# Loading q and k in 72-token runs from batch 3 on, so that the copies out of their transposes write unit steps

## The chip, the core and the metric

The kernel runs on one core of a Trainium2 chip. The metric is the device time of one execution in microseconds (us). Executions have a state: "slow" ones are longer at a lower granted TensorE clock, or over 1.5% above the fastest of the same kernel; comparisons here use fast runs. Engines: PE is TensorE (PEld its weight loads), DVE is VectorE, ACT is ScalarE, POOL is GpSimd, SP is SyncE, which issues DMAs here.

## The reference

Causal attention with a bias from a running sum, then a mixer that works first along the tokens (low rank) and then along the channels. Shapes: 8 batches, 8 heads, 576 tokens, head size 64, model width 512, hidden width 2048. Cut to what matters:

```python
scores = scale * q @ k.T                                 # per batch and head, causal
cum    = cumsum(maximum(s, 0), axis=-1)
scores = where(causal, -1e9, scores + minimum(-(cum_i - cum_j), 0))
x      = softmax(scores) @ v                             # heads side by side: (8, 576, 512)
u      = x + (x.T @ U @ V).T                             # mix along the tokens, rank 32
out    = u + maximum(u @ w_ch1, 0) @ w_ch2               # mix along the channels
```

## The kernel before

Heads go in pairs, n = 0..31, four pairs to a batch. For each pair, q and k are loaded with tokens on partitions, transposed by PE into PSUM (four 72x128 pieces per head and tensor; each piece holds two tokens' head rows, one in partitions 0-63 and one in 64-127), and copied as bf16 to `slot`, from which the score matmuls read. There are four such copies for a pair: two heads times two partition halves (`par`).

```python
def load_qk(b, h, n):                       # one run of 8 tokens (2 KB of fp32) per partition and head
    for dst, src in ((q_t[b], q), (k_t[b], k)):
        nc.gpsimd.dma_start(
            out=dst[:, ds(h, n), :],
            in_=src[b, ds(h, n)].rearrange("h (p t) d -> p h (t d)", p=TP),      # TP = 72
        )

def copies(n, hh, par):                     # which engine copies; DVE mostly
    b = n // PB
    on_act = hh == (n == 4) and ((n in (0, 1, 4, 8, 9) or n > 8 and n % PB == 2) or n == 2 and par == 0)
    return nc.scalar.copy if on_act else nc.vector.tensor_copy

def transposes(n):
    ... # cut: bias rows for slot by DMA; 16 PE transposes (line L280) into tps[hh], a PSUM bank per head
        dst = slot[0:D, hh, 0 : 2 * S].rearrange("p (c m t two) -> p c m t two", c=2, t=4, two=2)
        for par in range(2):
            copies(n, hh, par)(             # line L297
                dst[:, :, :, :, par],
                tp[par * D : par * D + D].rearrange("p c t m -> p c m t"),
            )
```

Row p of the load holds tokens 8p to 8p+7. So a transposed piece has every eighth token in its columns, and a copy must interleave: it writes every second bf16 element of `slot` and reads PSUM in steps of 72 elements.

The mixer's matmuls (128x512, lines L608 and L618) are woven between the attention steps in a fixed program order. The mix along the tokens (`seqmix`, L451 to L496) adds `xT`, a transpose of x made by DMA (24 transposes in the trace). All of q, k and v come through one DMA queue, fed by POOL. Loads of batch b+1 are issued once batch b-1's last transposes are done (POOL waits for such transposes four times in the trace of before, 114.1 us in all).

The softmax here doesn't subtract the row's maximum and nothing guards it: scores larger than these inputs give would overflow.

## Time and profile before

| | before |
|---|---|
| time, median of the runs beside after | 376.39 us |
| PE busy, whole span | 368.5 of 374.9 us |
| PE busy, 86 to 300 us (batches 3 to 7, mostly) | 213.46 of 214.00 us |
| `slot` copies, ns each | DVE 802, ACT 801 |
| packets on the DMA queue of q, k, v | 50,880 |

From the page, part 1: busy time of each engine, its share of the span, and its instructions.

```profile
PE 368.5 (98%) x3583; PEld 211.5 (56%) x3583; DVE 213.7 (57%) x446; ACT 200.8 (54%) x301; POOL 69.4 (19%) x108
```

The windows view: length of the window, then for each engine busy us (and instructions), then granted clock, DMA share and GB/s.

```profile
86.00:300.00 214.00, 213.46 (x2213) 124.87 (x2211) 138.37 (x293) 121.52 (x185) 20.41 (x25) 1.00 0.78 89
```

PE is full in the stretch in which the change acts; DVE is busy for 138 us of 214 and ACT for 122. A full PE is not by itself a proof, since matmul ends are modelled and a short wait can hide in them. The timeline agrees with PE as the limit all the same: four 128x512 matmuls hold PE for 0.86 us, and the next group starts at once (four start at 120.64 us, the next group at 121.50).

The view of tile `slot`, its copies (duration in ns as min/median/max, first and last start), and the line of the queue that POOL feeds (packets, MB, share of the time of 16 engines):

```profile
L297 DVE COPY slot<-pwork x105: 780/802/814, 8.2 to 275.2; 64x576 bf16<-64x576 bf16 x105
L297 ACT COPY slot<-pwork x23: 783/801/814, 6.9 to 259.7; 64x576 bf16<-64x576 bf16 x23
```

```profile
q0 software_dynamic: 50880, 18.44, 54.5%
```

### The profile page before, as it was taken

How to read it: one execution, taken by the hardware profiler on the slowest of the kernel's cores; microseconds unless marked ns; L12 is line 12 of the kernel's file. 1: busy time of each engine (PE TensorE's matmuls, PEld its weight loads, DVE VectorE, ACT ScalarE, POOL GpSimd, SP SyncE). 2: the span in 40 equal slices, each digit the busy share in tenths (PEclk: the TensorE clock that was granted, in tenths of full speed). 3: DMA queues.
4: the chain of work that ended last, by engine and by line, in shares of the span. 5: the costliest groups of instructions: out<-in, count | busy, mean ns of one | idle time of the engine just before them, and what ended most of it. 6: DMA issues, size and time to landing. Idle time of an engine off the chain costs nothing.

```text
span 374.9 us, 8505 instructions
## 1 busy us (share of the span) xinstructions
PE 368.5 (98%) x3583; PEld 211.5 (56%) x3583; DVE 213.7 (57%) x446; ACT 200.8 (54%) x301; POOL 69.4 (19%) x108
## 2 busy tenths in 40 slices
PE   8999999999999999999999999999999999999996
PEld 4675666666655556556656665666565544444443
DVE  7876777587668665876477756875573142002011
ACT  3875965757841777067814782368535610621610
POOL 8997436014002300140005000000000000000000
PEclk9999999999999999999999999999999999999999
DMA  7999999999948991699169923220223015302002
GB/s 109 166 206 205 175 173 134 179 124 138 89 55 138 172 78 26 127 164 119 20 117 151 135 34 87 79 63 17 51 81 92 19 35 120 71 30 84 0 30 84
DMA packets 89774, 37.29 MB, mean 99 GB/s; under 512 B 71112, under 2 KB 84136, under 8 KB 89736
## 3 DMA queue, kind: packets, MB, share of 16 engines
q0 software_dynamic: 50880, 18.44, 54.5%
q1 hardware_dynamic: 38856, 18.31, 27.2%
q8 instruction: 28, 0.46, 0.5%
q14 instruction: 10, 0.08, 0.1%
HBM read 37.25 MB, written 9.70 MB: 125 GB/s over the span
## 4 chain that ended last, share of the span: by engine, by line
PE 91%; ACT 4%; DVE 2%; issue 1%; DMA 1%; ACTq 0%; POOLq 0%
PE pwork L618 32%; PE pwork L608 31%; PE pscore L362 10%; PE pwork L422 8%; PE pwork L280 4%; ACT slot L297 2%; PE pscore L324 1%; DVE slot L297 1%; DMA q_sd<-in_q_dram 1%; PE pwork L655 1%; PE pscore L608 1%; ACT pT L388 1%; PE pscore L496 1%; ACT pT L377 0%; PE pwork L362 0%
## 5 line engine op out<-in xcount | busy, mean ns | idle before, releaser
L608 PE MATMUL pwork<-uT,w_sb 128*128 128x512 bf16 x560 | 135.6, 379 | 0.6 <-ACT pT L394 0.2
L618 PE MATMUL pwork<-w_sb,hT 128*128 128x512 bf16 x560 | 135.1, 379 | 0.3 <-DVE slot L297 0.3
L640 ACT ACTIVATE hT<-pwork 128x512 bf16<-128x512 f32 x140 | 84.8, 610 | 73.8 <-PE pwork L608 73.7
L297 DVE COPY slot<-pwork 64x576 bf16<-64x576 bf16 x105 | 84.0, 800 | 10.5 <-PE pwork L280 7.8
L377 ACT ACTIVATE pT<-pscore 128x1024 bf16<-128x1024 f32 x56 | 56.2, 1029 | 60.4 <-PE pscore L362 60.3
L608 PEld LDWEIGHTS <-w_sb 128*128 128x128 bf16 x576 | 51.0, 98 | 50.2 <-issue 1.2
L618 PEld LDWEIGHTS <-hT 128*128 128x128 bf16 x560 | 49.2, 98 | 49.2 <-issue 1.9
L362 PE MATMUL pscore<-slot 68*128 68x320 bf16 (+1 forms) x500 | 54.6, 246 | 0.2
L362 PEld LDWEIGHTS <-slot 68*128 68x128 bf16 x564 | 41.5, 97 | 22.9 <-issue 1.3
L678 DVE TENSOR_TENSOR o_sb<-pwork,u_sd 128x512 f32<-128x512 f32 x31 | 21.4, 689 | 57.3 <-PE pwork L618 56.7
L307 DVE TENSOR_TENSOR pT<-pT,keep 128x512 bf16<-128x512 bf16 (+1 forms) x81 | 28.7, 354 | 39.6 <-ACT pT L394 23.6
L422 PEld LDWEIGHTS <-pT 128*128 128x128 bf16 x870 | 33.1, 98 | 11.0 <-issue 0.3
L422 PE MATMUL pwork<-v_slot,pT 128*128 128x65 bf16 x870 | 35.3, 193 | 0.0
L432 DVE TENSOR_TENSOR x_sb<-pwork,rec 128x320 bf16<-128x320 f32 x64 | 31.5, 492 | 2.2
L107 POOL DMA_DIRECT2D q_sd<-in_q_dram x13 | 10.2, 782 | 117.4 <-PE pwork L280 114.1
L173 POOL DMA_DIRECT2D v_slot<-in_v_dram x36 | 30.4, 864 | 7.3 <-DMA w_sb<-in_moe_w_ch_dram 3.3
L388 ACT ACTIVATE pT<-pscore 128x1024 bf16<-128x1024 f32 x29 | 30.3, 1044 | 1.9 <-PE pscore L362 1.0
L431 DVE RECIPROCAL rec<-pwork 128x5 f32<-128x5 f32 x64 | 12.3, 192 | 24.6 <-PE pwork L422 24.1
L297 ACT COPY slot<-pwork 64x576 bf16<-64x576 bf16 x23 | 18.4, 801 | 7.3 <-PE pwork L280 6.6
L280 PEld LDWEIGHTS <-q_sd 72*128 72x128 bf16 x256 | 14.6, 98 | 9.9 <-DMA q_sd<-in_q_dram 1.0
L280 PE MATMUL pwork<-identity,q_sd 72*128 72x72 bf16 x256 | 18.4, 197 | 0.1
L280 PE MATMUL pwork<-identity,k_sd 72*128 72x72 bf16 x256 | 18.0, 197 | 0.0
(106 smaller groups left out, 194.7 us busy)
## 6 DMA issues: line engine op xcount, KB each, us to landing
out_dram<-o_sb SPq DMA_DIRECT2D x35, 256.0 KB
w_sb<-in_moe_w_ch_dram POOLq DMA_DIRECT2D x4, 1024.0 KB, 13.1
v_slot<-in_v_dram POOLq DMA_DIRECT2D x28, 128.0 KB, 15.8
q_sd<-in_q_dram POOLq DMA_DIRECT2D x5, 576.0 KB, 10.4
k_sd<-in_k_dram POOLq DMA_DIRECT2D x5, 576.0 KB, 14.5
q_sd<-in_q_dram POOLq DMA_DIRECT2D x4, 288.0 KB, 9.0
k_sd<-in_k_dram POOLq DMA_DIRECT2D x4, 288.0 KB, 15.3
q_sd<-in_q_dram POOLq DMA_DIRECT2D x4, 144.0 KB, 5.4
```

The source lines that it names most:

```text
L173: nc.gpsimd.dma_start(out=vt[:rows_t, t, :, 0:D], in_=v[b, :, ds(t * 128, rows_t), :].rearrange("h p d -> p h d"),)
L280: nc.tensor.transpose(tps[hh][:, c, t2, :], src[:, 2 * hp + hh, ds(t2 * 128, 128)], identity[:TP, :TP],)
L297: copies(n, hh, par)(dst[:, :, :, :, par], tp[par * D : par * D + D].rearrange("p c t m -> p c m t"),)
L307: nc.vector.tensor_tensor(dst, dst, keep[:, :, 0:w].to_broadcast([128, n_tiles, w]), op=ALU.min)
L362: nc.tensor.matmul(dst, lhsT=slot[0:KA, hh, ds(S + j * 128, 128)], rhs=slot[0:KA, hh, lo:hi], start=True, stop=True,)
L377: nc.scalar.activation(pT[:, hh, 0:1024], near, EXP, scale=scale)
L388: nc.scalar.activation(pT[:, :, 1024:1536], mid.rearrange("p (a b) -> p a b", a=2), EXP, scale=scale)
L422: nc.tensor.matmul(po[:, i, :], lhsT=pT[:, hh, ds(place(j, i), 128)], rhs=vt[:, j, h, :], start=(j == 0), stop=(j == i), skip_group_check= ...
L432: nc.vector.tensor_tensor(x_sb[:, hp, :, ds(hh * D, D)], po[:, :, 0:D], rec.to_broadcast([128, 5, D]), op=ALU.mult,)
L608: nc.tensor.matmul(f1, lhsT=w1_sb[:, kt, ds(nf * 128, 128)], rhs=u[:, kt, :], start=(kt == 0), stop=(kt == 3),)
L618: nc.tensor.matmul(f2, lhsT=hT[:, nf, ds(i * 128, 128)], rhs=w2_sb[:, nf, :], start=(nf == 0), stop=(nf == NF - 1 and not more), skip_grou ...
L640: nc.scalar.activation(hT[:, nf, :], f1, RELU)
```

## The change

Intent: from batch 3 on, load so that row p holds tokens p, 72+p, 144+p, and so on. Then a transposed piece has 72 consecutive tokens in its columns, and a copy reads and writes unit steps. That VectorE does such a copy faster was the author's assumption, which the trace of before does not show; 454 ns against 802 were measured afterwards. The price: the runs that a load reads shrink from 2 KB to 256 B, so there are eight times as many. Bytes, matmuls and their order stay.

```diff
+    def in_runs(b):
+        return b > 2
+
     def load_qk(b, h, n):
         for dst, src in ((q_t[b], q), (k_t[b], k)):
-            nc.gpsimd.dma_start(
-                out=dst[:, ds(h, n), :],
-                in_=src[b, ds(h, n)].rearrange("h (p t) d -> p h (t d)", p=TP),
-            )
+            if in_runs(b):
+                nc.gpsimd.dma_start(
+                    out=dst[:, ds(h, n), :].rearrange("p h (t d) -> p (h t) d", t=TT),
+                    in_=src[b, ds(h, n)].rearrange("h (t p) d -> p (h t) d", p=TP),
+                )
+            else:
+                ... # as before
@@ transposes
-            dst = slot[0:D, hh, 0 : 2 * S].rearrange("p (c m t two) -> p c m t two", c=2, t=4, two=2)
+            dst = slot[0:D, hh, 0 : 2 * S]
             for par in range(2):
-                copies(n, hh, par)(
-                    dst[:, :, :, :, par],
-                    tp[par * D : par * D + D].rearrange("p c t m -> p c m t"),
-                )
+                src = tp[par * D : par * D + D]
+                if in_runs(b):
+                    by_run = dst.rearrange("p (c t two m) -> p c t two m", c=2, t=4, two=2)
+                    copies(n, hh, par)(by_run[:, :, :, par, :], src)
+                else:
+                    ... # as before
```

More of the change, by code (lines that the diff above doesn't have):

```diff
@@ L103, in alloc_qk @@
         k_t[b] = loads.tile([TP, H, TT * D], BF16, tag="k_sd", name="k_sd")
+    def in_runs(b):
+        return b > 2
     def load_qk(b, h, n):
         for dst, src in ((q_t[b], q), (k_t[b], k)):
-            nc.gpsimd.dma_start(
-                out=dst[:, ds(h, n), :],
-                in_=src[b, ds(h, n)].rearrange("h (p t) d -> p h (t d)", p=TP),
-            )
+            if in_runs(b):
[4 more added lines that the diff above has]
+            else:
+                nc.gpsimd.dma_start(
+                    out=dst[:, ds(h, n), :],
+                    in_=src[b, ds(h, n)].rearrange("h (p t) d -> p h (t d)", p=TP),
+                )
     def ones(ap):
@@ L294, in transposes @@
             tp = tps[hh]
-            dst = slot[0:D, hh, 0 : 2 * S].rearrange("p (c m t two) -> p c m t two", c=2, t=4, two=2)
+            dst = slot[0:D, hh, 0 : 2 * S]
             for par in range(2):
-                copies(n, hh, par)(
-                    dst[:, :, :, :, par],
-                    tp[par * D : par * D + D].rearrange("p c t m -> p c m t"),
-                )
+                src = tp[par * D : par * D + D]
[3 more added lines that the diff above has]
+                else:
+                    in_turn = dst.rearrange("p (c m t two) -> p c m t two", c=2, t=4, two=2)
+                    copies(n, hh, par)(
+                        in_turn[:, :, :, :, par], src.rearrange("p c t m -> p c m t")
+                    )
             yield
```

## The prediction

> **What bounds the kernel.** TensorE. The page gives PE 368.5 us busy of a 374.9 us span at granted clock 1.0. The windows view, from 86 to 300 us (most of batches 3 to 7), has PE busy 213.46 of 214.00 us: 0.54 us idle. The waits view there lists one PE wait (0.2 us, on ACT) and, for weight loads, 0.4 us on a copy of `ux`, none on `slot`. The timeline shows groups following without gaps (four 128x512 matmuls in 0.86 us), so little waiting hides in modelled ends.
>
> **Removed.** The `slot<-pwork` copies (64x576, bf16, PSUM to SBUF) take 802 ns on DVE. For batches 3 to 7 there are 20 head pairs x 4 copies; 10 run on ACT, 70 on DVE. [...] Estimate: the two `o_sb` adds of 128 and 384 elements took 290 and 558 ns, so about 1.05 ns an element[...]. Total: 70 x 0.30 = 21 us of DVE busy, 213.7 -> about 193.
>
> **Added.** Each q or k load of a batch goes from 576 runs of 2 KB (packets of 1024 B written) to 4608 runs of 256 B (128 B written), as v has: 10 loads x 4032 = 40,320 more packets, queue 0 from 50,880 to about 91,200. [...] 1024 B packets ran at about 195 per us, 128 B ones at 450 to 1,200 per us. So q plus k of a batch should take about 18 us (10 to 27) instead of 6 to 8, and the whole load about 28 us instead of 18. PE's instructions are unchanged.
>
> **On the critical path?** Almost none of either. DVE's 21 us lie beside a full PE; at most some tenths of 0.54 us can come back. Loads for batches 4 to 7 are issued at 83, 119, 158 and 196 us; their first transposes are 36 to 45 us later, their values later still, so 28 us fits. Tightest is batch 3: issued at 56 us behind a backlog, packets flow from about 61 us, first transpose at 89 us; I expect q and k by about 80. Longer traffic beside stores and DMA transposes may cost tenths.
>
> **Predicted: 376.2 us, range 375.2 to 378.0; faster by over 2%: 0.01, within 2%: 0.96, slower by over 2%: 0.03.**
>
> **What would show each step.** Right: group `slot<-pwork` on DVE splits into about 35 copies at 802 ns and 70 near 500 ns, ACT's unchanged; DVE busy near 193 us; PE busy still about 368.5; queue 0 near 91,000 packets, its share of the engines up by half or more (54.5% -> 80 to 110%); landing of q and k for batches 3 on 15 to 30 us after issue. Wrong: copies still near 800 ns [...]; PE idle over 1 us between 86 and 300 us; a weight-load wait on q or k at about 89 us.
>
> **What would make it wrong.** Slower: 128 B packets at 350 per us or fewer, so batch 3's k lands after 89 us and stalls PE by some us. Faster: PE waits hidden behind modelled matmul ends that shorter copies release; no room for over 1 us.

The forecast came to 0.30 us less for each copy (802 to about 500 ns), 70 x 0.30 = 21 us less of DVE busy, and 376.2 us. The terms behind the 0.30 us were an assumption that no copy in the trace of before could confirm. The packet rates are of that trace: in single microseconds, 191 to 204 packets of 1,024 B (from 34 to 38 and from 45 to 52 us), and 391 to 1,210 of 128 B (from 39 to 43 and from 68 to 76 us, with packets of other sizes between).

## The result

| | before | after |
|---|---|---|
| time, median | 376.39 us (375.9 to 376.65, 4 runs) | 376.08 us (375.1 to 376.3, 4 runs) |
| ratio of fast runs, 95% interval | | 0.9988 (0.9968 to 1.0009) |
| DVE busy | 213.7 us | 189.5 us |
| `slot` copies from batch 3 on, ns | DVE 802, ACT 801 | DVE 454, ACT 634 |
| packets on the load queue | 50,880 | 104,640 |
| q and k of one batch: issue of q to landing of k (batch 4) | | 18.1 us |

Here and below a ratio is the mean time of one kernel's fast runs over that of the other's of the same rounds, so it is not quite the ratio of the medians.

The time is the same within noise, though every local effect took place. After, in the views shown of before (the new copies have line L309, the old ones L312):

```profile
PE 364.1 (98%) x3524; PEld 210.9 (56%) x3583; DVE 189.5 (51%) x446; ACT 199.1 (53%) x301; POOL 83.5 (22%) x108
```

```profile
L309 DVE COPY slot<-pwork x70: 438/454/460, 89.2 to 272.9; 64x576 bf16<-64x576 bf16 x70
L312 DVE COPY slot<-pwork x35: 786/803/814, 8.2 to 84.4; 64x576 bf16<-64x576 bf16 x35
L312 ACT COPY slot<-pwork x13: 783/801/808, 6.6 to 78.4; 64x576 bf16<-64x576 bf16 x13
L309 ACT COPY slot<-pwork x10: 632/634/635, 104.5 to 258.2; 64x576 bf16<-64x576 bf16 x10
```

```profile
q0 software_dynamic: 104640, 18.49, 83.7%
```

Seventy DVE copies became 348 ns shorter, which is 24 us, and DVE's busy time fell by just that: 213.7 to 189.5. PE's 364.1 us is not a gain: this trace lost 59 matmul records (3,524 of 3,583). A second trace of the same kernel (label e3_after_again) is complete; its windows view:

```profile
86.00:300.00 214.00, 213.78 (x2233) 125.30 (x2232) 115.17 (x294) 120.55 (x186) 31.86 (x27) 1.00 1.13 90
```

PE is busy for 213.78 of 214 us. VectorE has 23 us more to rest in this window, and the engine that sets the pace has the same work.

The loads did get slower and still landed in time. In after's view of DMA issues between 50 and 62 us (the last column is us from issue to landing) are the tightest ones, those of batch 3:

```profile
q_sd<-in_q_dram POOLq DMA_DIRECT2D x1, 576.0 KB, 14.2
k_sd<-in_k_dram POOLq DMA_DIRECT2D x1, 576.0 KB, 17.9
```

Its k was issued at 59.0 us, so it landed at 76.9 us; its first transposes began at 88.6 us. There were 11.7 us to spare.

### The profile page after: what moved, and what is told of

Read it like the earlier page. It is cut to its first block, busy times and chain, and to the rows that moved or that the text cites. A ratio compares the mean times of both kernels' runs of the same rounds, so it can differ in the third digit from the quotient of the medians.

```text
span 373.4 us, 8446 instructions
## 1 busy us (share of the span) xinstructions
PE 364.1 (98%) x3524; PEld 210.9 (56%) x3583; DVE 189.5 (51%) x446; ACT 199.1 (53%) x301; POOL 83.5 (22%) x108
## 3 DMA queue, kind: packets, MB, share of 16 engines
q0 software_dynamic: 104640, 18.49, 83.7%
## 4 chain that ended last, share of the span: by engine, by line
PE 91%; DVE 3%; ACT 2%; issue 2%; DMA 1%; ACTq 0%
PE pwork L632 31%; PE pwork L622 31%; PE pscore L376 10%; PE pwork L436 8%; PE pwork L289 4%; DVE slot L312 1%; PE pscore L338 1%; PE pwork L669 1%; PE pscore L622 1%; PE pwork L465 1%; DMA hT<-in_s_dram 1%; ACT pT L402 1%; PE pscore L510 1%; ACT pT L391 0%; PE pwork L376 0%
## 5 line engine op out<-in xcount | busy, mean ns | idle before, releaser
L622 PE MATMUL pwork<-uT,w_sb 128*128 128x512 bf16 x533 | 134.0, 379 | 1.7 <-ACT pT L408 0.2
L632 PE MATMUL pwork<-w_sb,hT 128*128 128x512 bf16 x531 | 129.9, 379 | 1.8 <-DVE slot L312 0.3
L309 DVE COPY slot<-pwork 64x576 bf16<-64x576 bf16 x70 | 31.7, 453 | 5.9 <-PE pwork L289 5.3
L312 DVE COPY slot<-pwork 64x576 bf16<-64x576 bf16 x35 | 28.1, 802 | 6.3 <-PE pwork L289 4.4
L111 POOL DMA_DIRECT2D q_sd<-in_q_dram x5 | 11.2, 2235 | 87.0 <-PE pwork L289 86.0
L289 PE MATMUL pwork<-identity,q_sd 72*128 72x72 bf16 x256 | 18.1, 196 | 0.5 <-DMA q_sd<-in_q_dram 0.4
```

The source lines that it names most:

```text
L289: nc.tensor.transpose(tps[hh][:, c, t2, :], src[:, 2 * hp + hh, ds(t2 * 128, 128)], identity[:TP, :TP],)
L309: copies(n, hh, par)(by_run[:, :, :, par, :], src)
L312: copies(n, hh, par)(in_turn[:, :, :, :, par], src.rearrange("p c t m -> p c m t"))
L622: nc.tensor.matmul(f1, lhsT=w1_sb[:, kt, ds(nf * 128, 128)], rhs=u[:, kt, :], start=(kt == 0), stop=(kt == 3),)
L632: nc.tensor.matmul(f2, lhsT=hT[:, nf, ds(i * 128, 128)], rhs=w2_sb[:, nf, :], start=(nf == 0), stop=(nf == NF - 1 and not more), skip_grou ...
```

## The experiments

Theory P: PE is full in the changed stretch, so neither the faster copies nor the slower loads matter. Rival C: both matter, and one gives back what the other gains. Both say that the sum is nought; doing one part alone tells them apart.

### e1: the loads alone, first attempt

The result is kept right: the copies take elements in the old order but go to the new places.

```diff
-                    copies(n, hh, par)(by_run[:, :, :, par, :], src)
+                    copies(n, hh, par)(
+                        by_run[:, :, :, par, :].rearrange("p c t m -> p c m t"),
+                        src.rearrange("p c t m -> p c m t"),
+                    )
```

> The loads of the change with copies that still write (and read) non-unit steps; the result stays right. Theory P (TensorE is full, so neither part matters): 376.0 to 376.8 us, 104,640 packets on queue 0, slot copies on DVE at 750 to 850 ns, PE idle under 1 us from 86 to 300 us. Rival C (the faster copies gain something and the loads lose about as much, so the sum is nought): clearly slower than before, by 1 us or more.

Measured: 508.72 us (506.51 to 513.56), ratio 1.349. This would be rival C's win, but it is not a test of the loads. The copies, expected at 750 to 850 ns, took 2.6 us:

```profile
L309 DVE COPY slot<-pwork x70: 2558/2586/2633, 90.2 to 408.8; 64x576 bf16<-64x576 bf16 x70
L309 ACT COPY slot<-pwork x10: 2592/2609/2638, 120.0 to 384.5; 64x576 bf16<-64x576 bf16 x10
```

They write in steps of 144 elements (288 B), where the old copies write in steps of 4 B. The experiment had brought in a new cost of its own. The test was done again as e5, and the step got its own runs (e4, e11).

### e2: the copies alone

The fast copies with the old loads. The q and k tokens of batches 3 to 7 land in a wrong order. (The comparison still passed as correct: q and k are drawn small, so the bias dominates the scores, and its rows keep their order. This run says nothing for the correctness of such a kernel.)

```diff
-            if in_runs(b):
+            if False:
                 nc.gpsimd.dma_start(     # in load_qk
```

> The fast copies with the old 2 KB loads; tokens of batches 3 to 7 land in a wrong order, so the result is wrong on purpose. Theory P: within 0.5 us of the after kernel, 375.5 to 376.4 us, DVE copies 454 ns and ACT copies 634 ns as after, 50,880 packets. Rival C: faster than before by 1 us or more.

Measured: 377.76 us median, 375.39 to 381.61, ratio 0.9987 (0.9928 to 1.0047). On this chip some executions were granted a clock of 0.98 to 0.99, so the times scatter. The three of these runs at a clock of 0.999 or more have a mean of 375.64 us, against 376.72 for the nine such runs of before. The median lies outside the expected 375.5 to 376.4 us because of those clocks; the three runs at full clock (375.39, 375.39, 376.14) fit it to 0.11 us. Their mean lies 1.08 us below that of before, right at the 1 us that rival C asked for, so times alone do not decide; the traces do better, below.

### e3: after once more

> The after kernel once more, for the size of a possible gain below the noise. Theory P: ratio 0.998 to 1.000, interval about 0.001 wide on each side; no theory expects over 0.5%.

Measured: 375.75 us median, ratio 0.9965 (0.9914 to 1.0017). The interval is wider than expected, for the same reason. The five runs at full clock have a mean of 375.68 us, as e2.

### e5: the loads alone, with the old copies

The new loads, and the old copy pattern at its 802 ns; tokens in a wrong order, as in e2.

```diff
-                if in_runs(b):
+                if False:
                     by_run = ...         # in transposes; the old pattern is used throughout
```

> Replaces the first run as the test of the loads alone, since that run's copies came out at 2.6 us instead of 0.8 us. Here batches 3 to 7 are loaded in 72 token runs, but the copies keep the old access pattern, 802 ns on DVE; the tokens of q and k land in a wrong order on purpose. Theory P (TensorE full, loads land in time): as before within 0.5 us, 104,640 packets, PE idle under 1 us from 86 to 300 us. Rival C (the loads lose what the copies gain): slower than before by 0.5 us or more.

Measured: 376.47 us (before 376.65), ratio 1.0007 (0.9972 to 1.0041). Queue and copies are as intended:

```profile
q0 software_dynamic: 104640, 18.49, 81.6%
```

```profile
L312 DVE COPY slot<-pwork 64x576 bf16<-64x576 bf16 x105 | 84.1, 801 | 10.8 <-PE pwork L289 8.0
```

Doubling the packets with nothing in return costs nothing that these runs resolve. Rival C's loss is not there.

### What the traces resolve: a gain of 0.95 us, it seems from ACT

The device times scatter by more than the question. But PE's order is fixed, so the distance in one trace between two given PE instructions shows what the changed stretch cost. From the first transposes of pair 10, just ahead of the change, to the last transposes of q and k (starts in us, from the timeline of weight loads):

| trace | pair 10 | last | distance |
|---|---|---|---|
| before | 77.67 | 273.55 | 195.88 |
| e5, loads only | 77.67 | 273.54 | 195.87 |
| e11, old loads, copies still at 800 ns | 77.34 | 273.24 | 195.90 |
| after | 77.11 | 272.04 | 194.93 |
| e3, after again | 77.77 | 272.70 | 194.93 |
| e2, copies only | 77.36 | 272.29 | 194.93 |

The copies save 0.95 us, a quarter of a percent, and the loads cost 0.01 us at most. So theory P holds to within 1 us. Rival C is right that the copies gain about 1 us, but fails because the loads lose nothing.

The gain comes in four pieces of about 0.24 us, at pairs 14, 22, 26 and 30 (at 22, from its second transposes to those of pair 23: before 182.59 to 194.44 us, 11.85; after 181.79 to 193.41, 11.62): where the transposes fall next to the mix along the tokens, and where one head's copies run on ACT. Pair 18 has both too and gains nothing (from its second transposes to those of pair 19, 11.61 us in both traces). At the four others, the matmul group behind the transposes takes a new `pwork` tile in PSUM; at pair 18 it goes on with a sum already begun (L618), and starts, in before, 0.26 us after the transposes do, where pair 22's group starts after 0.50 us. The timelines of before and then of after show pair 22 (start, duration, what, and idle time before it):

```profile
181.44 1.62 ACT L297 COPY slot<-pwork 64x576 bf16<-64x576 bf16 x2
182.71 0.20 PEld L280 LDWEIGHTS <-k_sd 72*128 72x128 bf16 x4
182.83 0.10 PEld L608 LDWEIGHTS <-w_sb 128*128 128x128 bf16 x1
183.11 0.53 PEld L608 LDWEIGHTS <-w_sb 128*128 128x128 bf16 x3 [0.18 <-issue]
183.11 1.02 PE L608 MATMUL pwork<-uT,w_sb 128*128 128x512 bf16 x4
```

```profile
180.65 1.28 ACT L309 COPY slot<-pwork 64x576 bf16<-64x576 bf16 x2
181.91 0.19 PEld L289 LDWEIGHTS <-k_sd 72*128 72x128 bf16 x4
182.04 0.57 PEld L622 LDWEIGHTS <-w_sb 128*128 128x128 bf16 x4
182.07 1.03 PE L622 MATMUL pwork<-uT,w_sb 128*128 128x512 bf16 x4
```

Before, ACT's two copies end at 183.06 us and the matmul group starts at 183.11, 0.24 us after PE could have begun it: the four weight loads are split in two. After, the copies end at 181.93, before PE gets there. The page showed almost none of this as PE idle time, because the modelled ends of the short transposes (0.29 us) cover the gap. That the matmuls wait for ACT, most likely for the `pwork` tile from which it copies, is read from these coincident times and from pair 18; no run changed ACT's copies alone.

### e4 and e11: which step makes a copy slow

e4 has the old loads and the old places, hence a right result, but walks the elements in the order in which they lie in PSUM. e11 also reads in unit steps, but writes every second element (tokens in a wrong order). Both use the loads of before.

```diff
+                    by_read = dst.rearrange("p (c m t two) -> p c t m two", c=2, t=4, two=2)   # e4
+                    copies(n, hh, par)(by_read[:, :, :, :, par], src)
```
```diff
+                    pairs = dst.rearrange("p (c t m two) -> p c t m two", c=2, t=4, two=2)     # e11
+                    copies(n, hh, par)(pairs[:, :, :, :, par], src)
```

> Old loads, old destinations, right result, but each copy walks its elements in the order in which they lie in PSUM (unit-step reads, writes 8 elements apart). It tells which side of the access made the copies slow. [...] DVE stays at 720 to 810 ns. If ACT's fall from 801 to 634 ns came from unit-step reads, ACT shows about 634 ns here; if from unit-step writes, about 800 ns. Time as before within 0.5 us by theory P.

> Old loads; each copy reads PSUM in unit steps and writes every second element (steps of 4 bytes), tokens in a wrong order on purpose. Against 802 ns (strided reads, 4-byte steps written), 454 ns (unit, unit) and 2,710 ns (unit reads, 16-byte steps written). If the write step alone decides: DVE about 800 ns, not 2,700. ACT at 634 ns would say that its gain comes from unit-step reads, at about 800 ns that it comes from unit-step writes. Time as before.

Measured, with the other patterns (median ns for 64x576 bf16 elements, PSUM to SBUF):

| kernel | step read | step written | DVE | ACT |
|---|---|---|---|---|
| after | 2 B | 2 B | 454 | 634 |
| e11 | 2 B | 4 B | 799 | 804 |
| before | 144 B | 4 B | 802 | 801 |
| e4 | 2 B | 16 B | 2710 | 2717 |
| e1 | 144 B | 288 B | 2586 | 2609 |

Between e11 and before only the read step differs, by a factor of 72, and the copies take the same time. So at this write step the reads don't matter; the write step decides. In all four slower cases both engines take nearly the same time.

Three gaps stand out: between unit steps and steps of 4 B written, 454 ns against 799 on DVE and 634 against 804 on ACT; and between steps of 4 B and of 16 B, where the copy took 3.4 times as long on both (2,710 and 2,717 ns). What causes them is not shown by these runs. No run wrote steps of 8 B, so where between 4 and 16 B the copies become so slow is not shown either. e4, a change of loop order alone, made the kernel 37% slower: 518.96 us, ratio 1.370 (1.363 to 1.378); e11 took 376.3 us in its one run. So e4's expectation, 720 to 810 ns and the time of before, was wrong (its condition: that for DVE only a unit-step write counts). Not all of this is waiting for copies: in every run of e1 and e4 the granted clock was 0.886 to 0.905, and the matmuls of the hidden layer took 420 ns on average, against 379. What lowered the clock was not tested. In e4 the chain of work that ended last is no longer PE's alone:

```profile
PE 58%; DVE 33%; ACT 5%; issue 4%
```

### e6: how much room VectorE has

Every copy of batches 3 to 7 in the kernel before is done twice.

```diff
-            for par in range(2):
+            for par in [0, 1] * (2 if b > 2 else 1):
```

> The kernel before, with every slot copy of batches 3 to 7 done twice (right result). It measures VectorE's slack: 70 more DVE copies of 802 ns are 56 us. From 86 to 300 us DVE is busy 138 of 214 us, and nearly all added copies fall there: 138 + 56 = 194 of 214 us. Theory P with slack in VectorE: between 376 and 390 us, since on average it still fits but the stage is then 90% full [...]. If VectorE had no slack, the time would rise by up to 56 us.

Measured: 392.84 us, ratio 1.0423 (1.0404 to 1.0442). This is above the expected 376 to 390 us. The added 70 DVE copies are 56 us, the added time 16 us. The windows view:

```profile
86.00:310.00 224.00, 209.76 (x2123) 122.57 (x2159) 188.61 (x360) 126.03 (x190) 21.07 (x26) 1.00 0.71 85
```

DVE is busy for 189 of 224 us, 84%, and PE already waits for it (PE's waits: us in total, times, longest; this trace lost 59 matmul records too):

```profile
PE pwork L608 <- DVE slot L297: 3.7, 4, 1.6
PE pwork L422 <- DVE slot L297: 3.6, 5, 0.8
```

VectorE was busy for 65% of the window before; part of its idle time was room, but not all of it. So the copies have their effect in this kernel mainly in one direction: longer ones cost, while shorter ones give only 0.95 us.

### e7 to e10: the same change where PE is not full

Half of the hidden layer's contraction and half of the output layer's are left out, so results are wrong; all else stays.

```diff
-            hidden(f1, u, nf, range(4))
+            hidden(f1, u, nf, (0, 3))
@@ outputs
         for nf in nfs:
+            if nf % 2 == 1 and nf < NF - 1:
+                if nf % 4 == 3 and nf < nfs[-1]:
+                    yield
+                continue
```

> The kernel before with half of the hidden matmuls (two of four contraction tiles) and half of the output matmuls left out: wrong result on purpose, TensorE relieved of some 110 us, all other engines' work kept. Theory P: 285 to 330 us, with PE no longer full from 86 us on and VectorE or ACT at its limit in parts.

> The same lightening of the after kernel. Theory P: once TensorE is not full, VectorE's 24 us are worth time: 5 to 24 us less than the light kernel before. A rival that VectorE's copies are never on the path, or that the loads cancel them: within 1 us of the light kernel before.

> The lightened kernel with the fast copies and the old 2 KB loads (wrong on purpose). In the lightened pair the after kernel gained nothing, though VectorE's share of the chain of waits fell from 16% to 7%; transposes xT by DMA took 9% of it instead of none. Theory D (in the lightened kernel the copies gain, and the longer small-packet loads give it back through late xT transposes): 285 to 292 us, 2 us or more below the light kernel before, no wait on xT. Rival E (in the lightened kernel ACT, the scores' exponentials and TensorE set the pace, so the copies gain nothing even alone): within 1 us of the light kernel before, 292.5 to 296 us.

> The lightened kernel with the loads in runs and the old copies (wrong on purpose). Theory D: 2 us or more slower than the light kernel before, 296 to 301 us, with waits on xT in the trace. Rival E: within 1 us of it.

| lightened kernel | loads | copies | ratio to before of its rounds (95%) | mean of its fast runs, us |
|---|---|---|---|---|
| e7 | old | old | 0.7821 (0.7789 to 0.7853) | 294.2 |
| e8 | new | new | 0.7825 (0.7798 to 0.7852) | 294.9 |
| e9 | old | new | 0.7728 (0.7699 to 0.7756) | 291.0 |
| e10 | new | old | 0.7868 (0.7844 to 0.7893) | 296.3 |

In e7's trace PE is busy for 260.8 us, against 368.5 of before (e7's lacks 50 matmul records). My expectation for e8, 5 to 24 us less, was wrong: with PE relieved, the whole change still gains nothing. Here rival C is right. The copies alone gain about 3 us; the interval of e9 lies below that of e7. The loads alone cost about 2 us, though the intervals of e7 and e10 just overlap, so the loss is likely rather than proven by time. What the loads do is seen in the waits of DVE between 80 and 240 us. First the light kernel before (e7), in which DVE has no wait on a DMA, then the first four lines of the light kernel after (e8); columns: us in total, times, longest.

```profile
DVE rec L431 <- PE pwork L422: 8.2, 17, 0.7
DVE pT L307 <- ACT pT L377: 7.5, 16, 1.0
DVE pT L307 <- ACT pT L394: 4.1, 12, 0.7
DVE uxT L460 <- PE pwork L451: 1.9, 4, 0.5
DVE o_sb L682 <- PE pwork L622: 0.7, 2, 0.4
DVE uT L476 <- PE pscore L496: 0.2, 1, 0.2
```

```profile
DVE pT L321 <- ACT pT L391: 23.7, 34, 1.4
DVE rec L445 <- PE pwork L436: 8.8, 17, 0.7
DVE pT L321 <- ACT pT L408: 5.4, 14, 0.7
DVE uT L490 <- DMA xT<-x_sb: 3.8, 3, 1.8
```

DVE's adds of the mix along the tokens now wait for `xT`, the transposes made by DMA. In e8's chain three of them stand on the path:

```profile
95.92 8.19 DMA xT<-x_sb
126.91 7.93 DMA xT<-x_sb
158.55 9.04 DMA xT<-x_sb
```

e10 shows the same wait (4.7 us) and e9 none; their two profiled executions were slow ones, so they only agree with the pair above, which is of fast ones. So the wait comes with the new loads; how they hold up `xT` is not shown. Between 80 and 240 us the packets' times sum to 1.13 times that of 16 engines in e7 and to 1.58 times in e8. In the full kernel there is no such wait: after's view of `xT` lists waits on PE alone, 2.4 us.

### e12: the new loads where DMA has no room

```diff
-        return b > 2
+        return b > 0
```

> The change from batch 1 on instead of batch 3. In the first 70 us the DMA engines are over 90% busy with weights and loads, and batches 1 and 2 are needed soon after their loads are issued. Theory P predicts that the cost of the loads shows where they do not land in time: 2 to 15 us slower than before, with waits of weight loads on q or k near 45 to 62 us. A rival that 8 times as many packets are harmless anywhere: within 1 us of before.

Measured: 380.55 us (377.67 to 382.68), ratio 1.0099 (1.0054 to 1.0144). The waits of PE's weight loads and, from the chain in order of time (start, duration), the load that came late:

```profile
PEld L289 <- DMA k_sd<-in_k_dram: 3.1, 2, 2.8
```

```profile
45.64 17.89 DMA k_sd<-in_k_dram
```

Up to 86 us the DMA engines are busy with weights and loads, 90% or more in each slice of before's page but the first. In the kernel before, this half of batch 2's k was issued at 40.9 us and landed 14.7 us later, at 55.6. Here it was issued 4.8 us later and took 17.9 us for the same 288 KB, and PE stood still for 2.8 us, up to 63.6 us, at the first transposes of batch 2. Eight times as many packets are not harmless everywhere. Starting at batch 3 keeps clear of this; why the line was drawn there is not known to me, and a start at batch 2, with batch 1 left as it was, was not tried.

No kernel tried here beats after by more than noise. The engine to relieve would be PE.

## Why the prediction was right

- **PE full, so same time.** Predicted 376.2 us, measured 376.08. That the two agree to 0.12 us is partly luck: the four runs spread over 1.2 us, and the traces show a gain of 0.95 us where the medians differ by 0.31. PE is busy for 213.78 of 214 us in the complete trace of after, and each half alone stays within 1 us.
- **The copies' size.** Predicted about 500 ns and DVE busy near 193 us; measured 454 ns and 189.5 us. A copy became 348 ns shorter, not 300, so the saving was 24 us, not 21. What made the copy faster is not shown; the 0.30 us was the assumption.
- **ACT's copies were said to stay unchanged: wrong.** They fell from 801 to 634 ns. e11 and before (804 and 801 ns, reads in steps of 2 and 144 B) show that the write step decides for ACT too. A small miss, but it is where the 0.95 us came from, as far as the timelines show. The prediction's main estimate of what could come back, some tenths of 0.54 us, was too small: it held that little waiting hides in modelled matmul ends, and 0.95 us did. Only its last paragraph allowed for this, with a bound of 1 us, which held.
- **Packets.** Predicted 91,200, measured 104,640. The 40,320 data packets came as predicted (5,760 of 1,024 B became 46,080 of 128 B). On top came 13,440 packets of 4 bytes, 1,344 for each of the ten loads (the trace lists 4,192 of them before and 17,632 after).
- **Loads in time.** Predicted: q and k of a batch in about 18 us, batch 3's by about 80 us. Measured: 18.1 us (batch 4), and 76.9 us. Single landings, predicted at 15 to 30 us after issue, were 10.3 to 14.2 us for q (faster) and 15.9 to 18.8 for k.
- **Late `xT` or stores.** Named as a possible cost of tenths of a microsecond. In the full kernel it cost nothing; in the lightened one it showed.

## What to carry to other kernels

Ask of a faster instruction which engine's full stretch it shortens: 24 us taken from an engine beside a full PE gave under 1 us, and that, as far as the timelines show, through a hand-off on a third engine. When two parts of a change push opposite ways, run each alone, also in a variant in which the bound engine is relieved; only there did this pair show both its gain and its price. And check the instruction's duration in the experiment first: a "neutral" loop order made the same copy 3.4 times as slow (2,710 ns against 802).
